# Attention, gated mixer and Fourier MLP on one core: the load pool's order and owners, the shared port's turn, and what goes to GpSimd

## The chip, the cores and the metric

The kernel runs on one core of a Trainium2 chip. The metric is the time of one execution on the device in microseconds. A core has five engines with queues of their own, each in order: TensorE (PE; its weight loads are PEld), VectorE (DVE), ScalarE (ACT), GpSimd (POOL) and SyncE (SP), which here issues most of the DMA transfers.

## The reference

Three blocks stand one behind the other, for 8 batches of 576 tokens (512 features, or 8 heads of 64).

```python
# attention with a feature map: phi(x) = [exp(p), exp(-p)], p = x @ w_phi - max|x @ w_phi|
q_p, k_p = phi(q), phi(k)
kv = einsum('bhsf,bhsd->bhfd', k_p, v); z = sum(k_p, axis=2)
x = (q_p @ kv) / (q_p . z + 1e-6)
# mixer: causal convolution of 5 taps for each feature, as a gate
gate = sigmoid(sum over k of conv_w[k] * xp[:, k:k + S])
x = (gate * (x @ w_val)) @ w_out
# Fourier transform over tokens and features, LayerNorm, MLP
u = x + real(fft(fft(x, axis=1), axis=2))
un = (u - mean(u)) / sqrt(var(u) + 1e-6)
out = u + relu(un @ w_ch1) @ w_ch2
```

## The kernel before

Matrix products are made in three passes: an operand is split into a rounded part hi (a copy by ScalarE) and the rest lo (a subtraction by VectorE or GpSimd), and hi x hi, hi x lo and lo x hi are added in PSUM. Nearly every operand therefore costs one ScalarE and one VectorE or GpSimd instruction.

The attention part (`run_attention`, up to about 300 us) is issued in an order written out by hand. All that follows is first noted as a list of operations (`op`, with the engines that may do it, the time that the planner allows for each, and the keys that it reads and writes) and then put into an order for each engine by `place_ops`, before anything runs. That order is fixed: on the chip each engine works through its own queue in it, waiting wherever data are not there yet.

`place_ops` first works out backwards when each operation is due, from the sum of the TensorE work (`place` for those whose place in the list counts). Then it goes forward: of all ready operations it takes the one that can start first, and of those on one engine the one due first. Two-way operations ("vp") may go to VectorE or GpSimd. One resource beside the engines is modelled, `free["x"]`: the port that GpSimd shares with VectorE's operations on two operands in SBUF; one of the two uses it at a time.

The noted part has these steps. For each batch b of the mixer: `note_x` splits x into `xh` (hi and lo), `note_taps` makes the convolution `acc` on VectorE, `note_V` multiplies by `wv` into the banks `val` and makes `gv`, `gs` (VectorE) and `ge` (hi, lo), `note_W` multiplies `ge` by `wo` and makes `fs` and `f`, `note_FD` transforms over features (banks `ps`, results `Y` and `rem`), and `note_SD` over tokens, into `u`, which is stored to `u_scr`. The sum of u and LayerNorm of the first MLP block is made inside the mixer by `ln_first`, in two halves of 462 tokens (`A`, `T0`, `s1`), each in three steps; the result is stored to `un_scr`. `note_mix` calls `in_place(next, ln0, None)` so many times after each batch. `note_sums` forms sums of weights on GpSimd in `ws` and stores them to `s_scr`.

The MLP works on 5 blocks of twice 462 (at last 456) tokens and in 8 steps of the hidden width, by a scheme with seven products in place of eight (`c1_units`: un times `r0`, into banks x, y, z; `c2_units`: h times `r1`, into cx, cy, added to `acc`). Its weights are loaded by SyncE into rings (`r0` of 10 tiles, `r1` of 6), and each tile is split again: hi on ScalarE, lo on VectorE or GpSimd (`r<-r`). `load_first` loads four tiles of un from `un_scr`; `prep_un` makes the other operands `un` by subtractions in `A` and splits them.

Memory is taken in stacks. When the mixer's right-hand pools end (`open_last`), the MLP's pool `lx` with the tiles of the list `LX` (14 of un, 10 of r0, c11, c12, c22) is laid over the space of ge0 (the `ge` of even batches), the g buffers (`gv`, `gs`, `acc`), `xh`, the two `xf` and `wv`. The tile framework makes the first write of a new tile wait for the last use of what lies beneath it, by real addresses. The planner learns of this only by `over(*tiles)`: it adds up sizes in the order of `LX`, compares them with the list `OLD` of (bytes, keys that end the use), and gives the keys to the loads as reads.

Of the kernel before, what the change touches and what calls it, by code (L numbers as in the profile page):

```python
# [13 lines left out]
ACTF = mybir.ActivationFunctionType  # L14
# [5 lines left out]
NB, NH, S, D, F = 8, 8, 576, 64, 128  # L20
# [3 lines left out]
NE = HS + 2  # L24
# [41 lines left out]
def attention_moe_mixer_kernel(  # L66
# [398 lines left out]
    wsteps = [(i, j) for j in range(NJ) for i in range(2)]  # L465
# [78 lines left out]
    def seq_pass(p, main, rem, a):  # L544
# [5 lines left out]
        else:  # L550
            mm(p, rem, sr[:, 2], start=False, stop=True)

    K = dict(h2="vp", un="vp", ln="vp", w="vp", lat=0.2, lnat=6, bw=0.003, dl=1.7, sq="a", su="a", ca=1, wl=1, win=0.0, marg=0.0, un0="vp", ln0="vp", w0="vp", t_lo="p", uf="vp")
# [7 lines left out]
    ops = []  # L561
    ring = None

    LX = [("un", 3, 0), ("un", 3, 1), ("un", 4, 0), ("un", 4, 1), "c11", ("un", 0, 1), ("un", 6, 1), "c12", ("un", 0, 0), ("un", 6, 0), ("un", 1, 0),
          ("un", 2, 0), ("un", 5, 0), ("un", 5, 1), "c22"] + [("r0", i) for i in (3, 4, 5, 6, 7, 8, 9, 0, 1, 2)] + [("un", 2, 1), ("un", 1, 1)]
    LX_SHAPE = {"un": [2, HB], "r0": [2, 2, 128], "c11": [HB], "c12": [HB], "c22": [HB]}
    OLD = [(8192, [("done", "V", n) for n in range(2)])] * 2 + [(4 * (S + 4) * 4, [("done", "x", b)]) for b in (NB - 2, NB - 1)]
    OLD += [(4 * S * 4, OLD[0][1])] * 2 + [(4 * S + 8 * NE + 16 * NE + 8 * S - 4 * S, [("done", "g", m) for m in (2, 3)])]
    OLD += [(16 * 4 * NE, [("done", "W", c, a) for c in range(4) for a in range(2)])]

    def over(*tiles):

        keys = []
        at = 0
        for t in LX:
            n = LX_SHAPE[t if isinstance(t, str) else t[0]]
            size = -(-4 * n[0] * (n[1] if len(n) > 1 else 1) * (n[2] if len(n) > 2 else 1) // 64) * 64
            if t in tiles:
                o = 0
                for m, k in OLD:  # L580
                    if o < at + size and at < o + m:
                        keys += [x for x in k if x not in keys]
                    o += m
            at += size
        return keys
# [87 lines left out]
    def o_act(o, x, func, cols, r, w, **kw):  # L673
        op("a", cols, lambda e: act.activation(out=o, in_=x, func=func, **kw), r, w, table=func if func in TABLES else None)
# [275 lines left out]
    def note_W(b, c):  # L950
        gh, gl = (later(("ge", b % 2, k)) for k in range(2))
        w = int(b == NB - 1)
        t = later(("x2", w))
        fs, f = tl["fs"], [later(("f", i)) for i in range(2)]
        for a in range(2):
            k, p = next(ring)
            p = p[:, 0:NE]

            def prod(e, a=a, p=p):
                for kk in range(4):  # L960
                    ws = slice(c * 128, (c + 1) * 128)
                    mm3(p, (wo[0][:, kk, ws], wo[1][:, kk, ws]), (gh[:, kk, a], gl[:, kk, a]), kk == 0, kk == 3)
            op("m", 0, prod, [("ge", b % 2, kk, i) for kk in range(4) for i in range(2)] + ["wo"], [k] + [("done", "W", c, a)] * (b == NB - 2), 12 * 0.134)
            if c >= 2:
                o_tt("v", fs[:, a], t[:, c - 2, a], p, (ALU.add, ALU.subtract)[a], NE, [k, ("x2", w, c - 2, a)], [("fs", a)])
            if c == 2 and a == 0:
                r = later(("xr", b % 2))
                o_hi(r[0:1], p[0:1], NE, [k], [("xr", b % 2, 0)])
                o_lo("v", r[32:33], p[0:1], r[0:1], NE, [k, ("xr", b % 2, 0)], [("xr", b % 2, 1)])
            o_act(t[:, c, a], p, ACTF.Copy, NE, [k], [("x2", w, c, a)])  # L970
        if c >= 2:
            c0 = c - 2
            fk = [("fs", 0), ("fs", 1)]
            o_hi(f[0][:, c0], fs, 2 * NE, fk, [("f", c0, 0)])
            o_lo(K["t_lo"], f[1][:, c0], fs, f[0][:, c0], 2 * NE, fk + [("f", c0, 0)], [("f", c0, 1)])
        if c == 2:
            q0 = 32 * (b % 4)
            o_act(later("r256")[q0:q0 + 1], t[0:1, 2], ACTF.Copy, 2 * NE, [("x2", w, 2, 0), ("x2", w, 2, 1)], [("r256", b % 4)])
# [79 lines left out]
    def note_mix():  # L1058
        rings = [[(("ps", i), later(("ps", i))) for i in range(n)] for n in (4, 5)]
        nonlocal ring  # L1060
        ring = cycle(rings[0])
        sums = iter(range(len(wsteps)))
        SUMS = [(1, 0, 1, 0, 1)] * 5 + [(1, 0, 0, 0, 0), (0,) * 5]

        def add_sums(n):
            for i in range(n):
                k = next(sums, None)
                if k is not None:
                    in_place(note_sums, k)

        ln0 = chain(ln_first(0), ln_first(1))
        tail = note_tail()
        next(tail)
        for m in range(4):
            note_taps(0, m)
            note_V(0, m)
            next(tail, None)
        for b in range(NB - 1):
            note_x(b + 1)
            for i, c in enumerate((0, 2, 1, 3)):  # L1080
                if i < 3:
                    note_taps(b + 1, i)
                    note_V(b + 1, i)
                note_W(b, c)
                add_sums(SUMS[b][i])
            add_sums(SUMS[b][4])
            note_taps(b + 1, 3)
            note_V(b + 1, 3)
            if b == NB - 2:
                ring = cycle(rings[1])  # L1090
                break
            note_FD(b)
            note_SD(b)
            for k in range((0, 1, 1, 2, 1, 1, 0)[b]):
                in_place(next, ln0, None)
        drain(ln0)
        b = NB - 2
        for n in range(RING[0]):
            note_weights(0, n)
        load_first()  # L1100
        note_FD(b)
        for c in (0, 2, 1, 3):
            note_W(b + 1, c)
        note_SD(b)
        note_FD(b + 1)
        note_SD(b + 1)
        prep_un(0, K["un0"])
# [28 lines left out]
    free = dict.fromkeys("mvapdxw", 0.0)  # L1136

    def place_ops():
        n = len(ops)
# [26 lines left out]
        due = [0.0] * n  # L1166
# [7 lines left out]
        for _ in range(2):  # L1174
# [14 lines left out]
            while heap:  # L1189
                late, i = (-k for k in heapq.heappop(heap))  # L1190
# [35 lines left out]
        behind = 0.0  # L1226
        table = ACTF.Exp
        for _ in range(n):
            best = None
            for e, q in ready.items():  # L1230
                cand = []
                for i in q:
                    d = ops[i][0]
                    if any(left_by[e][:max(part[i], at_part[e])]):
                        continue
                    t = first(i, e)
                    if e == "p" and "v" in d:
                        ahead = sum(ops[j][0]["v"] for j in ready["v"] if j != i and due[j] <= due[i] and at[j] <= t + 0.5)
                        if t + d["p"] > max(max(free["v"], at[i]) + ahead + d["v"], due[i] + behind + d["v"] - K["marg"]):
                            continue  # L1240
                    cand.append((i, t))
                if not cand:
                    continue
                t0 = min(t for i, t in cand)
                i, t0 = min(((i, t) for i, t in cand if t <= t0 + K["win"]), key=lambda c: (due[c[0]], c[0]))
                if best is None or t0 < best[0]:
                    best = t0, e, i
            t0, e, i = best
            for q in ready.values():
                q.discard(i)  # L1250
            part[i] = at_part[e] = max(part[i], at_part[e])
            for j in succ[i]:
                part[j] = max(part[j], part[i])
            for k in ops[i][0]:
                left_by[k][last[i]] -= 1
            free[e] = t0 + ops[i][0][e]
            if e == "p" or e == "v" and ops[i][5]:
                free["x"] = free[e]
            if e == "a":
                table = ops[i][8] or table  # L1260
            if e == "m":
                behind = t0 - due[i]
            start[i], end[i] = t0, free[e] + ops[i][4]
            if ops[i][10]:
                free["w"] = max(free["w"], free[e]) + K["bw"] * ops[i][10]
                end[i] = free["w"] + K["dl"]
            order.append((i, e))
            for s in succ[i]:
                at[s] = max(at[s], end[i] + lat * ("m" not in ops[i][0] or "m" not in ops[s][0]))
                left[s] -= 1  # L1270
                if not left[s]:
                    enter(s)
# [256 lines left out]
```

## Time and profile before

| | |
|---|---|
| median of 3 runs | 1355.23 us (1351.61 to 1355.76) |
| the profiled execution | 1354.46 us, its span 1352.7 us |
| TensorE busy (matmuls) | 1307.7 us, 97% of the span, 11952 matmuls |
| VectorE busy | 1178.4 us, 87% |
| ScalarE busy | 918.9 us, 68% |
| GpSimd busy | 822.2 us, 61% |
| mean granted TensorE clock | 0.99 |

The span runs from the first to the last instruction; the time of an execution also has what lies around it. Matmuls are pipelined, so a busy TensorE is not TensorE at its peak: the number of matmuls in a stretch and the granted clock (as a share of full speed) say more. An engine's idle time costs something only where another waits for it.

### The profile page before, as it was taken

The numbers are of one execution on the slowest core, as the hardware profiler recorded it, in microseconds if no ns is written. First come the engines' busy times: TensorE is split into PE (matmuls) and PEld (weight loads), VectorE is DVE, ScalarE is ACT, GpSimd is POOL, SyncE is SP. The second block draws the span as 40 slices with busy tenths as digits, with TensorE's granted clock in tenths as the row PEclk, the third lists the DMA queues.
The fourth block names the chain that finished last, engine by engine and source line by source line (L and its number), as shares of the span: only waits on it lengthen the run. The fifth ranks groups of instructions, "written<-read, shape, count | busy, mean of one in ns | idle before, by whom it ended". The sixth has DMA issues, their size and how long they took to land.

```text
span 1352.7 us, 30778 instructions
## 1 busy us (share of the span) xinstructions
PE 1307.7 (97%) x11952; PEld 1193.7 (88%) x11952; DVE 1178.4 (87%) x1867; ACT 918.9 (68%) x1872; POOL 822.2 (61%) x653
## 2 busy tenths in 40 slices
PE   7899999998999999989999999999999999999998
PEld 7788888987999999988888888888888888888997
DVE  6989988889898999869988999899988978998775
ACT  6888888866455555555877676776778676766662
POOL 4979798805666655525555765677657866673431
PEclk9999999999999999989999999999999999999999
DMA  7488888643343333243733473347333653346332
GB/s 255 143 267 263 285 280 298 209 175 130 126 141 134 127 126 133 96 154 125 236 103 106 134 231 104 102 134 237 104 108 105 211 160 102 107 112 204 103 90 87
DMA packets 151598, 214.63 MB, mean 159 GB/s; under 512 B 16790, under 2 KB 112278, under 8 KB 151452
## 3 DMA queue, kind: packets, MB, share of 16 engines
q1 hardware_dynamic: 147216, 203.21, 47.1%
q10 hardware_dynamic: 4236, 9.45, 1.8%
q8 instruction: 94, 1.54, 0.5%
q14 instruction: 52, 0.43, 0.1%
HBM read 165.63 MB, written 46.99 MB: 157 GB/s over the span
## 4 chain that ended last, share of the span: by engine, by line
PE 68%; DVE 22%; ACT 4%; issue 2%; DMA 2%; POOL 1%; SPq 0%; ACTq 0%; DVEq 0%; POOLq 0%
PE x L62 12%; PE cx L62 12%; PE cy L62 9%; PE ps L62 7%; PE y L62 6%; PE val L62 6%; DVE acc L62 4%; PE kv L62 4%; PE pj L62 4%; PE nm L62 3%; PE z L62 3%; PE yt L314 2%; DVE h L62 1%; DVE y L264 1%; DVE r L62 1%
## 5 line engine op out<-in xcount | busy, mean ns | idle before, releaser
L62 POOL TENSOR_TENSOR r<-r 128x256 fp32r<-128x256 f32 (+1 forms) x299 | 283.6, 966 | 214.3 <-ACT r L62 187.8
L62 ACT ACTIVATE r<-r 128x256 fp32r<-128x256 f32 (+1 forms) x420 | 193.0, 487 | 49.9 <-DMA r<-s_scr 48.4
L62 PE MATMUL x<-un,r 128*128 128x462 f32 (+1 forms) x960 | 223.0, 373 | 1.9 <-ACT c L62 1.9
L62 PE MATMUL cx<-h,r 128*128 128x462 f32 (+1 forms) x960 | 214.1, 371 | 3.5 <-DVE acc L62 3.5
L62 PEld LDWEIGHTS cx<-h,r 128*128 128x128 f32 x960 | 180.0, 188 | 25.6 <-DVE acc L62 5.2
L62 PEld LDWEIGHTS x<-un,r 128*128 128x128 f32 x960 | 180.7, 189 | 23.5 <-ACT c L62 2.6
L62 PE MATMUL cy<-h,r 128*128 128x462 f32 (+1 forms) x720 | 160.1, 371 | 0.0
L62 PEld LDWEIGHTS cy<-h,r 128*128 128x128 f32 x720 | 135.4, 188 | 15.2
L62 PE MATMUL val<-xh,wv 128*128 128x290 f32 x768 | 117.8, 302 | 7.4 <-DVE gv L62 3.8
L62 PEld LDWEIGHTS val<-xh,wv 128*128 128x128 f32 x768 | 108.6, 192 | 10.0 <-DVE gv L62 4.9
L62 PE MATMUL ps<-ge,wo 128*128 128x290 f32 x768 | 110.0, 301 | 6.2 <-DVE Y L62 5.4
L62 PE MATMUL y<-un,r 128*128 128x462 f32 (+1 forms) x480 | 114.4, 373 | 0.7 <-DVE h L62 0.7
L62 PEld LDWEIGHTS ps<-ge,wo 128*128 128x128 f32 x768 | 106.8, 193 | 6.6 <-DVE Y L62 5.7
L62 DVE SCALAR_TENSOR_TENSOR acc<-xf,cw,acc 128x576 f32<-128x576 f32 x128 | 105.1, 825 | 7.7 <-ACT acc L62 6.7
L62 PEld LDWEIGHTS y<-un,r 128*128 128x128 f32 x480 | 90.7, 190 | 11.7 <-DVE h L62 1.0
L261 DVE TENSOR_REDUCE m<-pj 128x8 f32<-128x1024 f32 (+1 forms) x80 | 88.7, 1108 | 12.2 <-PE pj L62 12.2
L62 ACT ACTIVATE h<-z 128x462 fp32r<-128x462 f32 (+1 forms) x120 | 66.3, 552 | 48.5 <-DVE z L62 44.0
L62 DVE TENSOR_TENSOR acc<-cx,acc 128x924 f32<-128x924 f32 (+1 forms) x80 | 88.7, 1109 | 11.7 <-PE cx L62 9.8
L62 PE MATMUL kv<-vraw,ke 128*64 128x66 f32 x2560 | 94.4, 226 | 2.0 <-DMA vraw<-in_v_dram 1.5
L62 DVE TENSOR_TENSOR r<-r 128x256 fp32r<-128x256 f32 (+1 forms) x121 | 78.9, 669 | 18.6 <-ACT r L62 18.4
L62 PE MATMUL pj<-wp,kqraw 64*128 64x128 f32 x1152 | 88.6, 291 | 5.3 <-DMA kqraw<-in_k_dram 4.5
L62 PEld LDWEIGHTS kv<-vraw,ke 128*64 128x64 f32 x2560 | 82.5, 138 | 12.7 <-ACT qe L317 1.7
(179 smaller groups left out, 2898.4 us busy)
## 6 DMA issues: line engine op xcount, KB each, us to landing
r<-s_scr SPq DMA_DIRECT2D x280, 128.0 KB, 2.1
r<-s_scr SPq DMA_DIRECT2D x140, 256.0 KB, 2.7
raw<-in_w_ch_dram SPq DMA_DIRECT2D x32, 512.0 KB, 4.8
vraw<-in_v_dram SPq DMA_DIRECT2D x16, 660.0 KB, 8.1
x_scr<-xT SPq DMA_DIRECT2D x32, 288.0 KB, 5.6
xf<-x_scr SPq DMA_DIRECT2D x8, 1152.0 KB, 9.0
u_scr<-u ACTq DMA_DIRECT2D x8, 1152.0 KB, 4.4
kqraw<-in_k_dram SPq DMA_DIRECT2D x15, 576.0 KB, 6.7
```

Source lines behind the costliest of these rows:

```text
L62: return lambda *a, **k: f(*(resolve(x) for x in a), **{n: resolve(x) for n, x in k.items()})
L261: nc.vector.tensor_reduce(out=m, in_=pv, axis=AX.X, op=ALU.max, apply_absolute_value=True)
L264: nc.vector.tensor_tensor(out=y, in0=pv, in1=m.unsqueeze(3).to_broadcast([128, 2, 2 * n, F]), op=ALU.subtract)
L314: nc.tensor.transpose(t[:, h, j, :], y[:, h, n + j, :], ident)
```

## The change

Five edits, all in the planner's input or in its rules; the operations and what they compute stay the same.

- The order of the tiles in `LX`, the list `OLD` (now from ge0 upwards to wv, with other sizes and keys) and the rounding of sizes (32 for 64 bytes).
- In `note_W` the copies of the last batch into x2 also read the key of the last stored sums.
- The steps of `ln_first` are called after batches 1, 1, 2, 3, 3, 4 in place of 1, 2, 3, 3, 4, 5.
- A two-way operation goes to GpSimd only where it would end before VectorE had worked off what is ahead and done it; before, it could also go there where it would end before it was due.
- Of operations that could start at the same time the planner takes the one that asked first (its engine free and its data there), not the first in the order of engines (TensorE, VectorE, ScalarE, GpSimd, DMA).

```diff
@@ -561,12 +561,12 @@
     ops = []
     ring = None
 
-    LX = [("un", 3, 0), ("un", 3, 1), ("un", 4, 0), ("un", 4, 1), "c11", ("un", 0, 1), ("un", 6, 1), "c12", ("un", 0, 0), ("un", 6, 0), ("un", 1, 0),
-          ("un", 2, 0), ("un", 5, 0), ("un", 5, 1), "c22"] + [("r0", i) for i in (3, 4, 5, 6, 7, 8, 9, 0, 1, 2)] + [("un", 2, 1), ("un", 1, 1)]
+    LX = [("un", 0, 1), ("un", 6, 1), ("un", 2, 1), "c11", ("un", 0, 0), ("un", 6, 0), ("un", 2, 0), ("un", 3, 0), ("un", 3, 1), ("un", 4, 0),
+          ("un", 4, 1), ("un", 5, 0), "c12", "c22", ("un", 5, 1)] + [("r0", i) for i in (9, 8, 0, 1, 2)] + [("un", 1, 1)] + [("r0", i) for i in (3, 4, 5, 6, 7)] + [("un", 1, 0)]
     LX_SHAPE = {"un": [2, HB], "r0": [2, 2, 128], "c11": [HB], "c12": [HB], "c22": [HB]}
-    OLD = [(8192, [("done", "V", n) for n in range(2)])] * 2 + [(4 * (S + 4) * 4, [("done", "x", b)]) for b in (NB - 2, NB - 1)]
-    OLD += [(4 * S * 4, OLD[0][1])] * 2 + [(4 * S + 8 * NE + 16 * NE + 8 * S - 4 * S, [("done", "g", m) for m in (2, 3)])]
-    OLD += [(16 * 4 * NE, [("done", "W", c, a) for c in range(4) for a in range(2)])]
+    V_DONE = [("done", "V", n) for n in range(2)]
+    OLD = [(13008, [("done", "W", c, a) for c in range(4) for a in range(2)]), (11640, [("done", "g", m) for m in (2, 3)]), (8 * 4 * S, V_DONE)]
+    OLD += [(16 * (S + 4), [("done", "x", b)]) for b in (NB - 1, NB - 2)] + [(16384, V_DONE)]
 
     def over(*tiles):
 
@@ -574,7 +574,7 @@
         at = 0
         for t in LX:
             n = LX_SHAPE[t if isinstance(t, str) else t[0]]
-            size = -(-4 * n[0] * (n[1] if len(n) > 1 else 1) * (n[2] if len(n) > 2 else 1) // 64) * 64
+            size = -(-4 * n[0] * (n[1] if len(n) > 1 else 1) * (n[2] if len(n) > 2 else 1) // 32) * 32
             if t in tiles:
                 o = 0
                 for m, k in OLD:
@@ -967,7 +967,7 @@
                 r = later(("xr", b % 2))
                 o_hi(r[0:1], p[0:1], NE, [k], [("xr", b % 2, 0)])
                 o_lo("v", r[32:33], p[0:1], r[0:1], NE, [k, ("xr", b % 2, 0)], [("xr", b % 2, 1)])
-            o_act(t[:, c, a], p, ACTF.Copy, NE, [k], [("x2", w, c, a)])
+            o_act(t[:, c, a], p, ACTF.Copy, NE, [k] + [("s",) + wsteps[-1]] * w, [("x2", w, c, a)])
         if c >= 2:
             c0 = c - 2
             fk = [("fs", 0), ("fs", 1)]
@@ -1091,7 +1091,7 @@
                 break
             note_FD(b)
             note_SD(b)
-            for k in range((0, 1, 1, 2, 1, 1, 0)[b]):
+            for k in range((0, 2, 1, 2, 1, 0, 0)[b]):
                 in_place(next, ln0, None)
         drain(ln0)
         b = NB - 2
@@ -1236,16 +1236,17 @@
                     t = first(i, e)
                     if e == "p" and "v" in d:
                         ahead = sum(ops[j][0]["v"] for j in ready["v"] if j != i and due[j] <= due[i] and at[j] <= t + 0.5)
-                        if t + d["p"] > max(max(free["v"], at[i]) + ahead + d["v"], due[i] + behind + d["v"] - K["marg"]):
+                        if t + d["p"] > max(free["v"], at[i]) + ahead + d["v"]:
                             continue
                     cand.append((i, t))
                 if not cand:
                     continue
                 t0 = min(t for i, t in cand)
                 i, t0 = min(((i, t) for i, t in cand if t <= t0 + K["win"]), key=lambda c: (due[c[0]], c[0]))
-                if best is None or t0 < best[0]:
-                    best = t0, e, i
-            t0, e, i = best
+                asked = max(free[e], at[i])
+                if best is None or (t0, asked) < best[0]:
+                    best = (t0, asked), e, i
+            (t0, _), e, i = best
             for q in ready.values():
                 q.discard(i)
             part[i] = at_part[e] = max(part[i], at_part[e])
```

## Rows read from the trace of the kernel before

**Rows 1.** The page's busy time, share of the span and instructions by engine.

```profile
PE 1307.7 (97%) x11952; PEld 1193.7 (88%) x11952; DVE 1178.4 (87%) x1867; ACT 918.9 (68%) x1872; POOL 822.2 (61%) x653
```

**Rows 2.** By stretch: us, PE, PEld, DVE, ACT, POOL, clock, DMA share, GB/s.

```profile
485.00:560.00 75.00, 69.73 (x507) 68.21 (x506) 71.40 (x124) 41.42 (x84) 40.99 (x36) 0.98 0.39 136
590.00:600.00 10.00, 5.06 (x40) 4.71 (x38) 1.91 (x3) 3.85 (x11) 0.00 (x0) 0.95 0.93 331
600.00:605.00 5.00, 4.50 (x18) 4.50 (x19) 4.91 (x10) 3.50 (x8) 2.17 (x1) 0.50 0.49 161
650.00:1300.00 650.00, 645.83 (x3075) 576.88 (x3074) 576.94 (x816) 461.72 (x967) 404.05 (x382) 1.00 0.47 139
```

**Rows 3.** Chain that ended last, 583 to 604: start, duration, what.

```profile
588.84 0.33 SPq L679
...
589.22 6.14 DMA un_scr<-A
...
595.43 3.53 DMA un<-un_scr
```

**Rows 4.** Waits of SyncE's queue, 570 to 600: total, times, longest.

```profile
SPq L679 <- DVE gs L62: 17.3, 1, 17.3
```

**Rows 5.** Timeline of VectorE: start, duration, instruction, idle time before.

```profile
504.52 1.41 DVE L62 TENSOR_TENSOR xh<-xf,xh 128x576 fp32r<-128x576 f32 x2
...
580.64 1.63 DVE L62 TENSOR_TENSOR A<-A,s 128x924 f32<-128x924 f32 x1
...
590.48 0.42 DVE L62 TENSOR_TENSOR Y<-ps,Y 128x258 fp32r<-128x258 f32 x1
598.99 1.12 DVE L62 TENSOR_TENSOR A<-un,un 128x924 f32<-128x924 f32 x1 [8.09 <-DMA un<-un_scr]
600.03 0.42 DVE L62 TENSOR_TENSOR Y<-ps,Y 128x258 fp32r<-128x258 f32 x1
```

**Rows 6.** Timeline of TensorE, the W matmuls and the first MLP pair.

```profile
575.76 8.23 PE L62 MATMUL ps<-ge,wo 128*128 128x290 f32 x60
...
600.50 12.29 PE L62 MATMUL ps<-ge,wo 128*128 128x290 f32 x72 [5.43 <-DVE Y L62]
...
639.79 2.51 PE L62 MATMUL x<-un,r 128*128 128x462 f32 x6 [1.89 <-ACT c L62]
```

**Rows 7.** DMA issues, 560 to 640: count, KB each, us to landing.

```profile
un<-un_scr SPq DMA_DIRECT2D x4, 462.0 KB, 4.4
```

**Rows 8.** Timeline of SyncE's queue and of ScalarE.

```profile
571.07 0.36 SPq L679 DMA_DIRECT2D s_scr<-ws  x1
...
593.04 0.98 ACT L62 ACTIVATE un<-un 128x924 fp32r<-128x924 f32 x1 [2.91 <-DMA un<-un_scr]
...
601.07 0.41 ACT L62 ACTIVATE x2b<-ps 128x290 f32<-128x290 f32 x1
```

**Rows 9.** Groups by shape, 350 to 585: count, busy, mean ns, idle before.

```profile
L62 POOL TENSOR_TENSOR ge<-gs,ge 128x580 fp32r<-128x580 f32 x20 | 29.6, 1484 | 25.4 <-ACT ge L62 25.2
...
L62 DVE TENSOR_TENSOR xh<-xf,xh 128x576 fp32r<-128x576 f32 x12 | 11.6, 992 | 0.0
...
L62 DVE TENSOR_TENSOR A<-A,s 128x924 f32<-128x924 f32 x4 | 5.8, 1475 | 0.0
L62 DVE TENSOR_TENSOR u<-x 128x574 f32<-128x574 f32 x5 | 5.5, 1103 | 0.0
L62 DVE RECIPROCAL s<-s 128x116 f32<-128x116 f32 x6 | 5.2, 870 | 0.1
```

**Rows 10.** Groups by shape, 650 to 1300: the weights' lo parts.

```profile
L62 POOL TENSOR_TENSOR r<-r 128x256 fp32r<-128x256 f32 x191 | 148.4, 789 | 91.6 <-ACT r L62 80.3 <-PE cy L62 3.7 <-DVE r L62 3.3
...
L62 POOL TENSOR_TENSOR r<-r 128x512 fp32r<-128x512 f32 x89 | 118.0, 1328 | 88.0 <-ACT r L62 78.6 <-PE x L62 3.5 <-PE cx L62 3.2
...
L62 DVE TENSOR_TENSOR r<-r 128x256 fp32r<-128x256 f32 x67 | 40.3, 607 | 6.3 <-ACT r L62 6.1
...
L62 DVE TENSOR_TENSOR r<-r 128x512 fp32r<-128x512 f32 x40 | 33.5, 842 | 9.5 <-ACT r L62 9.4
```

## The prediction

> **What bounds the kernel now.** I read the busy line of the page first, then busy time by stretch, then the chain of waits and the in-order queues at the weakest stretch. TensorE is busy 97% of the span [rows 1], so a change of order can only return idle TensorE time and time at a low clock. The attention part is written out by hand and the diff does not reach it. By stretch [rows 2]: from 485 to 560 TensorE idles 5.3 us while VectorE is busy 71.4 of 75, so there VectorE sets the pace. From 590 to 600 it idles 4.9 of 10 us, and from 600 to 605 its granted clock is 0.50, the lower of its two levels. From 650 to 1300 it idles 4.2 of 650 us: the MLP runs at TensorE's pace. The deepest hole is therefore the change from mixer to MLP, around 595.
>
> The chain [rows 3] says who made it: SyncE's queue moves at 588.84, then comes the store of A to un_scr (6.14 us), then the load of un (3.53 us), then VectorE. The wait list of the SyncE queue [rows 4] gives 17.3 us of waiting for VectorE's gs: the first un load stood at the queue's head for that long, and the store of A, ready since A's last multiplication ended at 580.64 + 1.63 = 582.27 [rows 5], stood behind it. On VectorE the subtraction A<-un,un then waits 8.09 us for that load; queued behind it is a small copy-out of Y (the lo part of a PSUM bank) at 600.03. TensorE needs that bank and waits 5.43 us until 600.50 [rows 6].
>
> Why gs? In the old order of the pool, un(0,1) starts 3712 x 4 + 1856 = 16,704 bytes in. The old list of what lay there puts it into an xf buffer, read out long before; the new list puts bytes 13,008 to 24,648 to the g buffers (gv, gs, acc). The trace waited for gs, so the new list is the true one. The tile framework always waited for the real neighbour; only the planner believed otherwise.
>
> **The change part by part.**
>
> *Order of the pool and true owners.* un(0,1), un(6,1), un(2,1) and c11 now end at 12,992 bytes, inside ge0, whose last readers are the W matmuls of batch 6, over at 575.76 + 8.23 = 583.99 [rows 6]. un(1,1) lies partly over wv, free once the last val matmuls are done, and those feed the gs that ended the wait at 588.84. So the first un loads can go at 584.0 and not at 588.84. One lands 4.4 us after its issue [rows 7]: 588.4; three of 462 KB one behind the other at the 331 GB/s of 590 to 600 [rows 2] need 4.2 us, so all are there by about 590. The subtraction starts about 590, not 598.99, directly behind the last Y of 590.48, and VectorE's 8.09 us of standing still go. Even with the store of A left where its data are ready, 582.27 + 6.14 + 3.53 gives 592, early enough for a bank that TensorE needs at 595.06. The hi tiles un(0,0), un(6,0), un(2,0), which ScalarE writes, now lie over g and wait for the last ge, which stands ahead of the Y of 590.48 in VectorE's queue [rows 5]; ScalarE already waited 2.91 us at this point, until 593.04 [rows 8]: no new cost. The weight tiles 0, 1, 2, 8 and 9 lie over xf and come free earlier; 3 to 7 lie over wv. Rounding to 32 and not 64 alters nothing: 3712, 1856 and 2048 are multiples of both.
>
> *The gain, on TensorE.* First the wait itself, 5.43 us. Second the clock: behind it the 72 W matmuls took 12.29 us; the 60 before took 8.23 us, which for 72 is 9.88, so 2.41 us were lost at the clock granted after the idle time. Sum 7.84 us. It isn't eaten by VectorE, though that is busy 4.91 of 5 us from 600 to 605: its 8.09 us come back at the same place, so its queue moves forward by as much as TensorE's. From 650 on TensorE is saturated and passes the gain to the end.
>
> *LayerNorm one block earlier.* The same instructions, moved: the last step is four reciprocals at 0.87 and two multiplications at 1.475 us [rows 9], 6.4 us of VectorE, with the store of A behind them in SyncE's queue. It leaves the time up to 582 and goes about a block back, into the stretch where VectorE sets the pace; steps of the same size leave that stretch in turn. Cost 0, covered by this exchange; without it up to 6.4 us on the path. It lets un_scr be stored before 584, which the 590 above wants.
>
> *Wait of the x2b copies for the last sums.* The last store of the sums was issued at 571.07, the first x2b copy began at 601.07 [rows 8]. Some 30 us of cover, 20 after the shift: 0.
>
> *GpSimd only when it ends before VectorE's backlog.* The test "or before it is due" goes, so fewer two-way operations go to GpSimd where VectorE is short of work. Where VectorE sets the pace its backlog is long and the answer stays the same. In the MLP TensorE is the bound and VectorE idles 73 of 650 us [rows 2], which is the cover. I take 0. Bounds: up to 5.3 us gained if the idle time of 485 to 560 goes with better placing; the losses are the rivals below.
>
> *The shared port to who asked first.* This changes only the order in which the two queues are filled. Bare, two xh subtractions took 1.41 us on VectorE [rows 5]; the mean over 350 to 585 is 0.99 [rows 9], so some 0.3 us of each is already waiting beside GpSimd. I take 0, as a turn that VectorE loses is one that GpSimd's f, which feeds TensorE, gains; the price if only the losses count is rival D.
>
> *What may come on top.* TensorE's wait of 1.89 us at 639.79 [rows 6], in the first MLP pair, may shrink as un is ready earlier against the mixer's end. I take 0, bound 1.9 us.
>
> **Sum.** The profiled execution took 1354.46 us (span 1352.7); the median of the runs is 0.77 us above it. 1355.23 - 7.84 = 1347.4, so 1347 us.
>
> **The rivals.**
>
> *Taken back (A).* The loads wait for something else, or the plan puts other loads ahead of them. Then the subtraction is at the head of VectorE's queue before its data again. For it: the queue is in order, and the planner's load times are its own numbers. Against it: every owner of the new places that I find is done by about 590.5. If 4 to 8 of the 7.84 us go back: 1351 to 1355, centre 1354.
>
> *More (B).* The stretch 485 to 560 loses its idle 5.3 us, and the first MLP pair its 1.9 us: 7.84 + 5.3 + 1.9 = 15.0 us at most, 1340; centre 1341. For it: the order there hangs on who gets which operation, and that is what the new test decides. Against it: VectorE has only 3.6 us idle in 75.
>
> *VectorE becomes the bound in the MLP (C), slower.* In 650 to 1300 GpSimd holds 191 weight subtractions of 256 and 89 of 512 columns, which cost VectorE 0.607 and 0.842 us each where it has them [rows 10]: 190.9 us for all 280, 0.682 each. VectorE has 73 us free, so this decides from 107 moved operations (38%) on. At half of them, 140: 95.5 - 73 = 22.4 us over, 1347.4 + 22.4 = 1370. For it: such splits have late due times, so little counts as backlog ahead of them. Against it: with VectorE 89% busy a new one seldom finds it free.
> A page bears on this price. The Trainium skill (GPSIMD Engine Reference, Engine selection) says that two-input elementwise work is about 2x slower on GpSimd than on VectorE. By it the 266.4 us that GpSimd spent would be 133 us on VectorE, and the point would lie at 55%. The rows show 789 against 607 ns and 1328 against 842 ns, only 1.3 and 1.6 times, so the sum goes by the rows.
>
> *VectorE loses the port (D), slower.* From 350 to 585 VectorE has 12 xh at 0.99 and 5 u of 574 columns at 1.10 us, both inputs in SBUF [rows 9], against a bare 0.7 of xh. If GpSimd's ge (1.48 us) now stands ahead of each, it waits up to 1.48 - 0.3 = 1.18 us more, 20 us for the 17, where VectorE sets the pace. Seven such waits eat the gain, ten make the kernel slower than before by 4 us. At all of them: 1347 + 20 = 1367.
> The Trainium skill (SBUF — State Buffer, Who interferes with whom) states that whichever of the two starts first holds the pair for its whole instruction and the other blocks. By it each lost turn costs the whole GpSimd operation; the rows show stretched means that agree, but no run here isolates one turn.
>
> **How the numbers follow.** Forecast 0.45, own range 1343 to 1351; taken back 0.22; more 0.15; C 0.11; D 0.07. No change and a change can be told apart at 0.3%, 4 us: below 1351.2 is faster, above 1359.3 slower. Faster 0.45 + 0.15 = 0.60, same 0.22, slower 0.18. The range has to leave out no more than 0.2: C and D (0.18) and the far end of B go; 1338 to 1359.
>
> **What would show it.** Right: the first un load leaves SyncE's queue near 584 and behind PE or a load, not behind gs; the store of A to un_scr lies well before it; VectorE's A<-un,un starts near 590 with little wait; no wait of TensorE for Y near 595 and a granted clock near 1.00 from 600 to 610; the MLP's stretches unchanged, 7 to 8 us earlier. Wrong: a wait of several us of VectorE or ScalarE for un remains (A); weight subtractions on VectorE rise past some 214 of 387 (107 are there now) with TensorE waiting for r or h (C); u, xh and ge grow longer on VectorE with TensorE's idle time from 485 to 560 above 5.3 us (D).

## The result and the profile after

The changed kernel takes 1340.63 us (median of four runs, 1340.23 to 1341.10), the kernel before 1353.42 us beside it (four runs, 1349.91 to 1355.76). The ratio is 0.991, with a 95% interval of 0.9888 to 0.9933: faster by 12.8 us. The forecast was 1347 us, a gain of 7.8. The profiled execution took 1340.58 us, its span 1338.8. The page's line of busy time, against [rows 1], shows the same work in a shorter span:

```profile
PE 1303.8 (97%) x11952; PEld 1190.6 (89%) x11952; DVE 1172.2 (88%) x1879; ACT 927.0 (69%) x1874; POOL 811.1 (61%) x641
```

The wait that the forecast is built on is gone. First the queue of SyncE, against [rows 3, 4]:

```profile
559.80 11.49 SPq L679 DMA_DIRECT2D r<-s_scr  x5
584.39 3.40 SPq L679 DMA_DIRECT2D un<-un_scr  x4
587.85 3.24 SPq L679 DMA_DIRECT2D r<-s_scr  x5
```

The four un loads leave from 584.39 on, one behind the other. No store of A stands between them, and the list of waits of this queue has no row for gs any more. VectorE's timeline, against [rows 5]:

```profile
590.85 0.75 DVE L62 TENSOR_TENSOR Y<-ps,Y 128x258 fp32r<-128x258 f32 x2
591.52 1.11 DVE L62 TENSOR_TENSOR A<-un,un 128x924 f32<-128x924 f32 x1
```

The subtraction follows the last Y with no idle time in the brackets, where 8.09 us stood before. In the kernel before, the second of these Y stood behind the subtraction; here both are ahead of it. TensorE's timeline, against [rows 6]:

```profile
592.06 13.04 PE L62 MATMUL ps<-ge,wo 128*128 128x290 f32 x96
...
628.57 1.53 PE L62 MATMUL x<-un,r 128*128 128x462 f32 x6 [0.73 <-DVE c L62]
631.52 1.53 PE L62 MATMUL x<-un,r 128*128 128x462 f32 x6 [1.43 <-ACT c L62]
```

The last 96 W matmuls are one piece of 13.04 us; before, they were 24, a wait of 5.43 us, and 72 that began at a low clock (0.50 from 600 to 605 [rows 2]).

To see all of the gain, I cut both spans at four marks that each trace has: the first val matmul (the mixer begins), the first and the end of the last 96 W matmuls, the first and the last start of cx (the MLP's second product). The table of busy time by stretch, columns as in [rows 2], first of the kernel before:

```profile
313.60:591.70 278.10, 265.60 (x2037) 260.29 (x2034) 251.30 (x464) 149.79 (x306) 158.75 (x145) 0.99 0.37 126
591.70:612.50 20.80, 15.37 (x98) 15.13 (x97) 12.98 (x16) 14.05 (x33) 7.85 (x4) 0.84 0.51 185
612.50:650.30 37.80, 35.41 (x201) 31.88 (x200) 33.15 (x58) 20.76 (x51) 16.71 (x15) 0.95 0.54 180
650.30:1347.60 697.30, 693.13 (x3303) 619.74 (x3301) 608.59 (x859) 481.35 (x1004) 415.66 (x392) 1.00 0.45 135
```

and of the changed one:

```profile
311.50:592.10 280.60, 267.80 (x2036) 260.55 (x2034) 250.22 (x470) 154.43 (x312) 152.10 (x142) 0.99 0.42 138
592.10:604.80 12.70, 12.70 (x97) 12.70 (x96) 12.20 (x12) 12.22 (x29) 9.67 (x6) 1.00 0.07 22
604.80:639.20 34.40, 32.24 (x194) 29.48 (x193) 31.58 (x54) 20.56 (x48) 20.32 (x18) 1.00 0.53 183
639.20:1333.70 694.50, 693.29 (x3308) 621.65 (x3307) 609.11 (x875) 486.53 (x1007) 405.65 (x379) 1.00 0.45 136
```

Below, the four stretches are called mixer, last W, transition and MLP. In this pair of profiled executions the last W is shorter by 8.1 us, the transition by 3.4 and the MLP by 2.8; the mixer is longer by 2.5, and it began 2.1 earlier, behind the attention part, which the diff doesn't reach (this start lies anywhere from 311 to 318 in the 14 traces of this study, which all have the same attention code). Sum: 13.9 us, the difference of the two spans. Of the 3.4, TensorE's idle time (37.80 - 35.41 = 2.39 and 34.40 - 32.24 = 2.16) explains 0.2 and the clock 1.9 (5% of 37.8); most of the rest is one group of six matmuls which now comes behind the first cx and so counts in the MLP. In the MLP the idle time fell from 4.17 to 1.21.

The weights' lo parts in the MLP, 650 to 1300, against [rows 10] (groups by shape):

```profile
L62 POOL TENSOR_TENSOR r<-r 128x256 fp32r<-128x256 f32 x197 | 162.4, 836 | 126.6 <-ACT r L62 123.4 <-PE cx L62 1.3 <-DMA r<-s_scr 1.3
L62 POOL TENSOR_TENSOR r<-r 128x512 fp32r<-128x512 f32 x85 | 115.7, 1363 | 91.8 <-ACT r L62 83.3 <-PE cx L62 5.2 <-PE y L62 2.7
...
L62 DVE TENSOR_TENSOR r<-r 128x512 fp32r<-128x512 f32 x43 | 32.7, 763 | 11.2 <-ACT r L62 11.1
L62 DVE TENSOR_TENSOR r<-r 128x256 fp32r<-128x256 f32 x63 | 27.6, 444 | 1.8 <-ACT r L62 1.8
```

VectorE has 106 of them, and had 107: nothing moved to it. Rival C did not happen. But each of the shorter ones takes 444 ns on VectorE and not 607, and 836 on GpSimd and not 789.

And VectorE's pace in the stretch from which rival B wanted 5.3 us, against [rows 2]:

```profile
485.00:560.00 75.00, 70.92 (x510) 68.98 (x509) 68.11 (x123) 42.54 (x81) 49.40 (x45) 0.98 0.41 136
```

TensorE idles 4.1 us there in place of 5.3. The measured time lies where rival B put it (1341), but not for B's main reason.

### The profile page after: what moved, and what is told of

It reads as the page before. It is cut to its first block, busy times and chain, and to the rows that moved or that the text cites. A ratio compares the mean times of both kernels' runs of the same rounds, so it can differ in the third digit from the quotient of the medians.

```text
span 1338.8 us, 30805 instructions
## 1 busy us (share of the span) xinstructions
PE 1303.8 (97%) x11952; PEld 1190.6 (89%) x11952; DVE 1172.2 (88%) x1879; ACT 927.0 (69%) x1874; POOL 811.1 (61%) x641
## 4 chain that ended last, share of the span: by engine, by line
PE 83%; DVE 10%; ACT 2%; POOL 2%; DMA 2%; issue 1%; SPq 0%; DVEq 0%; POOLq 0%; ACTq 0%
PE x L62 15%; PE cx L62 15%; PE cy L62 11%; PE ps L62 10%; PE y L62 8%; PE kv L62 5%; PE pj L62 5%; PE nm L62 4%; PE val L62 4%; PE z L62 4%; DVE acc L62 3%; PE yt L314 3%; PE xt L356 1%; DVE y L264 1%; DVE m L261 1%
## 5 line engine op out<-in xcount | busy, mean ns | idle before, releaser
L62 POOL TENSOR_TENSOR r<-r 128x256 fp32r<-128x256 f32 (+1 forms) x301 | 293.9, 994 | 244.0 <-ACT r L62 223.9
L62 PEld LDWEIGHTS pj<-wp,kqraw 64*128 64x128 f32 x1152 | 73.3, 192 | 18.2 <-issue 18.1
```

The costliest lines, as they stand in the source:

```text
L62: return lambda *a, **k: f(*(resolve(x) for x in a), **{n: resolve(x) for n, x in k.items()})
```

## The experiments

Medians are given with the ratio to the kernel before, run on the same chip in between. In all the diffs, "pool" means the new `LX` with the new `OLD` and its rounding. Lines of profiles are of the experiment's own execution.

**The pool alone.** `LX`, `OLD`, the rounding, and the key of x2b; the LayerNorm steps and both planner rules as before.

```diff
-    LX = [("un", 3, 0), ("un", 3, 1), ("un", 4, 0), ("un", 4, 1), "c11", ("un", 0, 1), ...
+    LX = [("un", 0, 1), ("un", 6, 1), ("un", 2, 1), "c11", ("un", 0, 0), ("un", 6, 0), ...
...
-    OLD = [(8192, [("done", "V", n) for n in range(2)])] * 2 + [(4 * (S + 4) * 4, ...
+    OLD = [(13008, [("done", "W", c, a) for c in range(4) for a in range(2)]), ...
```

> Only the pool's new order, its true owners, the rounding and the x2b key; LayerNorm's places and both planner rules as before. Theory P (the pool is the whole gain): 1340 to 1343 us, the first un load leaves the queue near 584, VectorE waits under 1 us for un. Rival S (shares): the pool gives the 8 us of the stall and of the slow clock, 1344 to 1347, the planner rules the other 4 to 5. Rival L (LayerNorm's earlier store is needed): the store of A still stands behind the loads of un from 584, VectorE waits 3 to 6 us and the time is 1347 to 1351.

Measured: 1346.45 us, 0.9938 (0.9915 to 0.996), a gain of 8.5. SyncE's queue:

```profile
579.90 0.32 SPq L679 DMA_DIRECT2D un_scr<-A  x1
581.97 3.40 SPq L679 DMA_DIRECT2D un<-un_scr  x4
```

Its stretches: mixer 277.0, last W 12.8, transition 38.1, MLP 696.9. Against before that is -1.1, -8.0, +0.3, -0.4. The predicted term of 7.84 us is here, at its place and in its size, and reaches the end whole.

**All but the pool.** The changed kernel with the old `LX`, `OLD` and rounding.

> The other half: LayerNorm one block earlier, the x2b key and both planner rules, with the pool's old order and old owners. Theory P: the first un load still waits for gs until about 589, but un_scr has been stored long before, so the load lands near 593 and VectorE's wait shrinks to some 2 to 4 us without going: 1347 to 1351. Rival S: the same and 4 to 5 us more from the rules, 1343 to 1346. If the wait is untouched: 1353 to 1355.

Measured: 1353.92 us, 0.9991 (0.9975 to 1.0007): no gain. The old places make the old wait in SyncE's queue, though A was stored long before:

```profile
558.96 0.33 SPq L679 DMA_DIRECT2D un_scr<-A  x1
...
593.53 3.06 SPq L679 DMA_DIRECT2D un<-un_scr  x4
```

```profile
599.27 1.12 DVE L62 TENSOR_TENSOR A<-un,un 128x924 f32<-128x924 f32 x1 [3.69 <-DMA un<-un_scr]
```

```profile
600.78 9.87 PE L62 MATMUL ps<-ge,wo 128*128 128x290 f32 x72 [1.04 <-DVE Y L62]
```

On VectorE a Y still stands behind the subtraction, as in the kernel before. So this trace shows what the late space costs when no store stands behind the load: VectorE waits 3.69 us and not 8.09, TensorE 1.04 and not 5.43, and the 72 matmuls then take 9.87 us and not 12.29. (The planner's rules differ from before as well.) The last W takes 14.0 us. But the transition takes 45.5 us, 7.7 more than before; TensorE's longest waits in it are 3.26 us for ScalarE's c and 2.86 us for VectorE's fs. Whether they come from the late loads isn't shown.

**True owners, old order.** `OLD`, rounding and the x2b key; the old `LX`. So memory is as before, and only the planner knows better.

```diff
-    OLD = [(8192, [("done", "V", n) for n in range(2)])] * 2 + ...
+    OLD = [(13008, [("done", "W", c, a) for c in range(4) for a in range(2)]), ...
```

> Only the true owners (and the x2b key), with the pool's old order. If the planner's false belief was the fault, it now puts the store of A ahead of the un loads and VectorE's other work ahead of A<-un,un: un loads still not before gs near 589, landing near 593, TensorE's wait of 5.4 us gone or under 2 us: 1345 to 1349. If the order itself (what lies beneath the first loads) is what counts: 1350 to 1354.

Measured: 1348.48 us, 0.9953 (0.9937 to 0.997). The queue, now with the store of A ahead of the load that must wait:

```profile
583.62 0.32 SPq L679 DMA_DIRECT2D un_scr<-A  x1
588.92 0.32 SPq L679 DMA_DIRECT2D un<-un_scr  x1
589.29 0.42 SPq L679 DMA_DIRECT2D r<-s_scr  x1
```

The load still waits for the old space, until 588.92, and yet the last W takes 12.7 us. But the plan changed on another engine too: the subtraction that waited at the head of VectorE's queue is now on GpSimd.

```profile
598.73 2.18 POOL L62 TENSOR_TENSOR A<-un,un 128x924 f32<-128x924 f32 x1 [5.79 <-DMA un<-un_scr]
```

It starts about as late as before (598.99; 5.4 us after the last W began, 7.3 before), still behind a wait for the load, but no Y stands behind it there; VectorE is through with these Y at 592.91. So a planner that reckons with the late load can keep TensorE from waiting although the data are late. That the store's place in SyncE's queue alone made the 8 us can't be read from this run. What the last W gains is not all kept: the transition takes 40.4 us, 2.6 more than before.

**New order, old owners.** `LX` with the rounding and the x2b key; the old `OLD`, which now describes a layout that isn't there.

```diff
-    LX = [("un", 3, 0), ("un", 3, 1), ("un", 4, 0), ("un", 4, 1), "c11", ...
+    LX = [("un", 0, 1), ("un", 6, 1), ("un", 2, 1), "c11", ("un", 0, 0), ...
```

> Only the pool's new order (and the x2b key), with the old, false owners. If what truly lies beneath the first un loads is what counts, they go at about 584 whatever the planner believes (it thinks of wv, free near 587): 1344 to 1348 us, no wait of TensorE for Y near 595. If the planner's knowledge is what counts, other operations now wait where it sees none (the hi tiles of un over g, the weight tiles 3 to 7 over wv): 1350 to 1354.

Measured: 1350.00 us, 0.9969 (0.9947 to 0.9991). The un loads leave only from 585.59 on, 2.7 us before the last W begins (7.7 in the changed kernel): weight loads stand ahead of them, and the queue waits 4.9 us for TensorE's val. VectorE waits 2.92 us for un, with the Y ahead of the subtraction. The last W takes 13.0 us, but TensorE then waits 5.0 us at 612 for VectorE's fs, and the transition is 43.1. Either half removes the hole; on the medians each is worth 5 to 6.5 us and both 8.5, but their intervals overlap.

**The store on another queue.** The kernel before with one edit: the store of A to un_scr is issued by ScalarE.

```diff
-        o_dma([(un_scr[k], tl["A"])], ak, [("un_scr", k)], 2 * HB)
+        o_dma([(un_scr[k], tl["A"])], ak, [("un_scr", k)], 2 * HB, "a")
```

> The kernel before, with the two stores to un_scr issued on ScalarE's queue in place of SyncE's. If the store stuck behind the un load makes the 8.1 us wait, it now goes at about 583, the second un load follows the first at once near 589.5 and lands near 594: VectorE's wait 3 to 4 us, TensorE's for Y under 1.5 us, 1346 to 1349. If the wait comes from elsewhere: 1352 to 1355.

Measured: 1350.45 us, 0.9975 (0.996 to 0.999). The store goes at 582.17 and the wait of 5.43 us for Y is gone. But this edit, too, put the subtraction on GpSimd, with the Y ahead on VectorE:

```profile
598.49 2.18 POOL L62 TENSOR_TENSOR A<-un,un 128x924 f32<-128x924 f32 x1 [8.83 <-DMA un<-un_scr]
```

The un loads leave at 591.41 and 593.29, and TensorE's timeline shows a new wait, and one where 1.89 us stood before:

```profile
608.41 2.35 PE L62 MATMUL ps<-ge,wo 128*128 128x290 f32 x12 [2.76 <-DVE xr L62]
...
641.45 1.52 PE L62 MATMUL x<-un,r 128*128 128x462 f32 x6 [2.10 <-ACT c L62]
```

Last W 16.0 and transition 40.2: 4.8 gained and 2.4 given back. On the medians the edit is worth 4.5 us, about half of the pool. As the plan moved the subtraction as well, the queue alone isn't tried by this run.

**No move of LayerNorm.** The changed kernel, with the steps of `ln_first` where they were.

```diff
-            for k in range((0, 2, 1, 2, 1, 0, 0)[b]):
+            for k in range((0, 1, 1, 2, 1, 1, 0)[b]):
```

> The changed kernel with LayerNorm's steps where they were. If the earlier store of un_scr isn't needed: 1339 to 1343 us, the store at about 580 to 583 and the un loads right behind it. If it is part of the gain: 1344 to 1348 and a wait of 2 us or more of VectorE for un.

Measured: 1341.87 us, 0.9902 (0.9878 to 0.9927), the changed kernel's time. The move is worth nothing that can be measured, either way.

**No rule of who asked first.** The changed kernel with the old tie: the first in the order of engines.

```diff
-                asked = max(free[e], at[i])
-                if best is None or (t0, asked) < best[0]:
-                    best = (t0, asked), e, i
-            (t0, _), e, i = best
+                if best is None or t0 < best[0]:
+                    best = t0, e, i
+            t0, e, i = best
```

> The changed kernel with the old tie rule (VectorE ahead of GpSimd when both could take the port). If the new turn is what fills the MLP better: 1343 to 1347 us. If it is worth nothing or costs in the mixer, where VectorE sets the pace from 485 to 560: 1337 to 1342.

Measured: 1341.77 us, 0.9902 (0.9873 to 0.9931): again the same. But not in the same places: mixer 275.5 in place of 280.6, transition 39.9 in place of 34.4. In these traces the rule moves time from one stretch to another.

**No backlog test.** The changed kernel with the old test for GpSimd.

```diff
-                        if t + d["p"] > max(free["v"], at[i]) + ahead + d["v"]:
+                        if t + d["p"] > max(max(free["v"], at[i]) + ahead + d["v"], due[i] + behind + d["v"] - K["marg"]):
```

> The changed kernel with the old test for GpSimd (also where it ends before it is due). Theory M (the last 3 to 4 us come in the MLP from VectorE and GpSimd being filled otherwise): 1343 to 1347 us, TensorE idle 3 to 4 us from 650 to 1300 as in the kernel before. If the test is worth nothing: 1339 to 1342.

Measured: 1349.30 us, 0.9951 (0.9932 to 0.9969), slower than either range expected: without this one line some 6 us of the change's gain are lost (0.9951 - 0.991 is 0.41%, 5.6 us). TensorE in the first MLP pair:

```profile
635.43 2.68 PE L62 MATMUL x<-un,r 128*128 128x462 f32 x6 [3.33 <-ACT c L62]
637.91 2.51 PE L62 MATMUL y<-un,r 128*128 128x462 f32 x6
640.21 2.05 PE L62 MATMUL x<-un,r 128*128 128x462 f32 x6
```

and what GpSimd did just ahead:

```profile
624.25 2.75 POOL L62 TENSOR_TENSOR u<-x2b 128x578 f32<-128x578 f32 x2 [2.90 <-DVE x2b L62]
626.97 4.44 POOL L62 TENSOR_TENSOR r<-r 128x256 fp32r<-128x256 f32 x5
```

Under the old test work that isn't due for long goes to GpSimd one piece behind the other. TensorE waits 3.33 us, and three groups of six then take 2.68, 2.51 and 2.05 us in place of some 1.4 (granted clock 0.50 from 635 to 640). The transition takes 40.7 us against 34.4; the mixer is 2.3 us shorter than in the changed kernel, the MLP 0.4 longer, and the mixer began 4.0 later. That GpSimd's row of five subtractions is what delayed TensorE is read from these two timelines, and not tried by itself.

**The backlog test alone.** The kernel before with this one line of the change.

```diff
-                        if t + d["p"] > max(max(free["v"], at[i]) + ahead + d["v"], due[i] + behind + d["v"] - K["marg"]):
+                        if t + d["p"] > max(free["v"], at[i]) + ahead + d["v"]:
```

> The kernel before with the new test for GpSimd alone. If the test works by itself: 1348 to 1351 us. If its gain lies in the first MLP pair and can only be had once the un loads come early, so that the stall at the loads hides it: 1352 to 1357, VectorE's wait for un still 5 us or more.

Measured: 1345.45 us, 0.9936 (0.9919 to 0.9953), ten runs from 1337.80 to 1349.91: a gain of 8.6, as much as the pool's and more than either range expected. The un stall is still there:

```profile
589.04 1.12 DVE L62 TENSOR_TENSOR A<-un,un 128x924 f32<-128x924 f32 x1 [7.94 <-DMA un<-un_scr]
```

and the gain is in the mixer and the MLP (windows at the marks and at the stretch of [rows 2]):

```profile
311.90:581.90 270.00, 263.98 (x2035) 258.68 (x2034) 250.92 (x478) 149.90 (x306) 139.69 (x131) 0.99 0.39 130
...
642.20:1335.50 693.30, 692.61 (x3303) 620.34 (x3302) 610.74 (x894) 482.26 (x1004) 378.14 (x356) 1.00 0.46 136
```

```profile
485.00:560.00 75.00, 74.72 (x565) 74.01 (x564) 73.39 (x140) 45.12 (x92) 43.91 (x40) 1.00 0.38 130
```

The mixer's idle TensorE time goes from 12.5 to 6.0 us and the stretch is 8.1 shorter; from 485 to 560 only 0.3 us are left idle. The MLP is 4.0 us shorter, the transition 2.4 longer. VectorE took over work (478 instructions and not 464, GpSimd 131 and not 145) and is busy no longer than before: 250.92 us against 251.30.

**Pool and backlog test.** The first and the last experiment together; LayerNorm and the tie as before.

> The pool's part and the new test for GpSimd, without the new tie rule and without LayerNorm's move. If these two are the whole change: 1339 to 1343 us, as the changed kernel, with a wait of TensorE in the first MLP pair of no more than 2.5 us. If the tie rule or LayerNorm's place is needed beside the test: 1344 to 1347, near the pool alone.

Measured: 1338.04 us (1334.24 to 1341.26), 0.9884 (0.9861 to 0.9906), a gain of 16.0, near the sum of 8.5 and 8.6. Mixer 271.1, last W 12.7, transition 38.4, MLP 694.1. It is the fastest version here, 2.6 us below the changed kernel, but the two intervals overlap, so the order of the two isn't settled. With it, four kernels have the pool and the test, and their stretches (one trace each) show what the other two edits do: the mixer takes 271.1 us with neither, 275.5 with LayerNorm's move, 279.3 with the tie rule and 280.6 with both; the transition takes 38.4, 39.9, 34.3 and 34.4. So the tie rule costs 5 to 8 us in the mixer and gives 4 to 5.5 back in the transition; LayerNorm's move costs 1 to 4 in the mixer.

**f's lo part open to VectorE.** The changed kernel with `t_lo` "vp" in place of "p".

```diff
-    K = dict(h2="vp", ..., un0="vp", ln0="vp", w0="vp", t_lo="p", uf="vp")
+    K = dict(h2="vp", ..., un0="vp", ln0="vp", w0="vp", t_lo="vp", uf="vp")
```

> The changed kernel, with f's lo part open to VectorE too (GpSimd alone before). If f's turn on GpSimd holds up the feature transforms in the mixer: 1335 to 1339 us, with less idle TensorE time from 350 to 560 than the 8.8 us now. If VectorE, which sets the pace there, only gets more work: 1341 to 1346.

Measured: 1349.39 us, 0.9956 (0.9936 to 0.9976): slower than the changed kernel, and than either range expected. TensorE, in the window from 485 to 560, waits on VectorE's f:

```profile
530.44 0.58 PE L62 MATMUL ps<-ft,f 128*128 128x258 f32 x1 [3.83 <-DVE f L62]
```

But by the marks the mixer takes 280.8 us, as in the changed kernel, so this wait isn't the loss. The loss is in the transition: 40.4 us, 6.0 more, with a wait of 3.67 us for VectorE's h. Why h comes late there wasn't tried.

**A longer look at the backlog.** The changed kernel, where work that is ready up to 2.0 us later counts as ahead.

```diff
-                        ahead = sum(ops[j][0]["v"] for j in ready["v"] if j != i and due[j] <= due[i] and at[j] <= t + 0.5)
+                        ahead = sum(ops[j][0]["v"] for j in ready["v"] if j != i and due[j] <= due[i] and at[j] <= t + 2.0)
```

> The changed kernel, counting as VectorE's backlog what is ready within 2 us and not 0.5: more goes to GpSimd, half way back to the old test. If the test's gain is that late work stays off GpSimd just before it is needed: 1343 to 1348 us, with a longer wait in the first MLP pair. If only the mixer's balance counts: 1337 to 1342.

Measured: 1341.43 us, 0.9904 (0.9884 to 0.9923): no difference from the changed kernel, though GpSimd then does 304 of the weights' lo parts from 650 to 1300 and not 282. The bare count of operations on GpSimd isn't what matters.

## Why the prediction was right, and where it was too small

**The stall.** Right, in place and size. The first un load was predicted at 584.0 and left at 584.39; the subtraction at about 590, directly behind the last Y, and began at 591.52 behind it; the wait of 5.43 us and the slow 72 matmuls were worth 7.84 us by the sum, 8.1 between the marks, and 8.5 on the medians with the pool alone. Rival A did not happen. One part of the reading was too narrow: I took the early release of the space for what matters. The wait came of three things together: a late load, a store stuck behind it, and a Y behind the subtraction in VectorE's queue. Without the store in the way (all but the pool) 1.04 of the 5.43 us are left; with the subtraction on GpSimd (true owners with the old order, and the store on another queue) nothing is left of this wait, though the data still come late. The pool's part ends the late load and puts both Y ahead, so its runs don't say which of the two would have done.

**The backlog test.** This is the step that failed: "Where VectorE sets the pace its backlog is long and the answer stays the same", and "I take 0". Alone, the line gives 8.6 us; within the whole change, some 6. My bound for it, 5.3 us of idle time from 485 to 560, was at the right place and too small. With the test alone 5.0 us of just this idle time went, but the mixer gained 8.1 and the MLP 4.0: I looked at 75 us of a mixer that is 278 us long and has 12.5 us of idle TensorE time [rows 2 shows only the weakest stretch], and left out the MLP. In the changed kernel itself this gain isn't in the mixer (idle 12.8) but in the transition (34.4 us, and 40.7 without the line). In the MLP I counted on VectorE's free time as cover and didn't ask what TensorE's own 4.2 idle us were: cut at the marks, they are 3.9 to 4.3 in the five kernels with both old rules, 0.7 to 2.4 in the seven with the new test, 3.0 in the one with the longer look, and 2.2 in the one with the new tie and the old test, so the tie, or LayerNorm's move, which that kernel also has, may have a part in it.

**What may come on top.** Mis-sized, and for a wrong reason: taken as 0, with a bound of 1.9 for a wait that un's earlier arrival might shorten. The wait hardly shrank (1.43 us in place of 1.89); what went is the low clock behind it, which the bound left out although the same sum charged 2.41 us for the clock behind the other wait. With the pool alone un comes as early, and the wait (2.12 us at 630.00) and the low clock behind it (0.66 from 630 to 635) are both there, so un's arrival isn't what did it. Transition and MLP together gave 6.2 us between the marks. With the 8.1 of the last W and less the mixer's 2.5 that is 11.8; the 2.1 of the earlier start make it the 13.9 of the two profiled executions, and the medians differ by 12.8.

**LayerNorm, x2b key, tie.** LayerNorm and tie at 0: borne out, each by leaving it out. The key of x2b was part of the kernel with the pool and wasn't tried by itself; its 30 us of cover were there (the first x2b copy waited for nothing in the trace after). Rival D was not seen by its signs (xh on VectorE takes 0.88 us on average from 350 to 585, and TensorE idles 4.1 us from 485 to 560), and without the tie rule the time is the same. But the mixer, D's stretch, is where the tie rule costs its 5 to 8 us. What I didn't expect is that the edits don't add. With the test but without the tie rule the mixer idles 6.0 to 9.7 us; with both, 12.8 to 13.1 (11.6 with the longer look). Without the pool, the test gives 8.6 us alone and nothing together with LayerNorm's move, the tie rule and the key of x2b. The stretches with the pool point to the tie rule; which edit spoils it without the pool, and by which operations, stays open: the planner's order changes everywhere when one rule does.

**The price of a weight subtraction on VectorE** (rival C). VectorE's share stayed the same, so the point of 107 moved operations wasn't put to the test. The price wasn't a constant: VectorE's own cost (27.6 + 32.7) / 106 = 0.569 us each after and (40.3 + 33.5) / 107 = 0.690 before (the prediction's 0.682 is the same with GpSimd's share of long ones). GpSimd against VectorE is now 836 to 444 and 1363 to 763, 1.9 and 1.8 times. The Trainium skill (GPSIMD Engine Reference, Engine selection) says about 2x; the trace after agrees with it better than the trace before, whose 607 and 842 ns I took for the sum.

**The range.** 1338 to 1359 holds 1340.6; the likeliest case's own, 1343 to 1351, does not. It was built around one term, with the others at 0: a gain of 7.8 us, where 12.8 were measured. That the stated range reaches down to the measured time is owed to rival B, and of B's two terms little came: 1.2 of the 5.3 us from 485 to 560, and 0.5 of the 1.9 us of wait. So the range held partly by luck.

## What to carry to other kernels

Where a hand-made planner feeds in-order queues, its idea of when reused memory comes free must be the memory's real layout: one load taken for ready can hold a finished store behind it, and the operation that waits for the load can hold others behind it in its own queue; together that cost 8 us on an engine two steps away. When a stall goes, look whether the data came earlier or whether the one that waits for them only stands elsewhere. Before an edit to a placing rule is costed at nothing because "the answer stays the same", count the idle time of the bound engine over the whole part that the rule governs, not in its worst stretch, and add to each wait the low clock behind it. Then try each edit both alone and left out: two here were worth nothing on the whole, and the other two (the pool with its key, and the test) made all of the gain.

## What the runs showed of the hardware

The length of a wait doesn't say by itself what TensorE's clock does behind it. Before, a wait of 1.89 us at 639.79 was followed by a granted clock of 0.66 from 640 to 645. With the test alone a wait of 2.11 us at the same place of the work (633.15) left it at 1.00 up to 645, and without the test a wait of 3.33 us was followed by 0.50 from 635 to 640. What else decides wasn't tried.

The same subtraction (256 columns, both operands in SBUF) took VectorE 607 ns on average in the kernel before and 444 in the changed one, without a change of shape; 730 in the kernel without the backlog test. Over the 14 traces the mean is 426 to 465 ns in the seven kernels where GpSimd was busy 365 to 396 of these 650 us, and 593 to 730 ns in the seven where it was busy 402 to 443. So the mean goes with the work on GpSimd, and such a mean from one trace isn't a fixed price; no run changes GpSimd's work and nothing else.

Runs of one kernel spread by up to 0.9% (the test alone, 1337.80 to 1349.91) and by as little as 0.06% (the four of the changed kernel). Some of it seems to lie ahead of anything edited: the first val matmul, behind an attention part whose code no edit touches, started anywhere from 311 to 318 us in the 14 traces. Single profiles can therefore differ by more than an edit is worth; stretches between marks and the medians decide.
